# Laying the sums of expert weights over the steps: one split a step, half-size weight units, and a second output product that runs on through the set-up of the pairs

## The chip, the core and the metric

The kernel runs on one core of one Trainium2 chip. The core has TensorE (PE, matmuls, with a weight load in front of each), VectorE (DVE), ScalarE (ACT), GpSimd (POOL) and SyncE (SP), which here only issues DMAs. Tiles live in SBUF, matmul results in the eight banks of PSUM, tensors in DRAM. Each engine works through its own list in order and waits on semaphores for the others; SP's list is the DMA queue, so a DMA that must wait holds back all those behind it. The metric is the device time of one execution, as the median of several runs.

## The reference

Eight batches of attention with 12 heads, 448 positions and head size 64, where the heads are mixed before and after the softmax, and behind it a gated layer without nonlinearity over all 3584 rows:

```python
scores = scale * np.matmul(q, k.transpose(0, 1, 3, 2))
scores = np.einsum('bhij,hg->bgij', scores, w_pre)
attn = softmax(scores)                       # along the last axis
attn = np.einsum('bhij,hg->bgij', attn, w_post)
x = (attn @ v)  # to rows of 768
a = x @ w1; b = x @ w2                       # 768 x 1024 each
out = (a * b @ w3) @ w_out                   # 1024 x 1024, 1024 x 768
```

The weights of the layer arrive in double precision and are converted in the kernel.

## The kernel before, in words

**The steps.** `run` walks through 366 steps `n`. A step takes ten query rows of all twelve heads (120 partitions) through one stage each of a pipeline: `fetch` of the raw scores four steps ahead, `split_r` into a high and a low part two steps ahead (DVE L201, POOL L202), `mix` one ahead (PE L209 to L211), `softmax` (DVE L218, ACT L221), and behind it `scale` (DVE L230 to L233) and `post` (PE L241, with the copy L247 on ACT that empties the bank). One `mix` ends each step, so the 360 matmuls of L211 mark the steps in the trace; all stretches below are cut at their ends. Scores of later batches (L174, L175, store L183) and the product with `v` (L272) are spread over the steps by tables. A step with `av` work has 48 matmuls of L272 and no background work.

**The background.** Between these, `advance` issues matmuls of a background generator. `shares` gives each step its number, so that `count` matmuls lie evenly between two steps. First w3 and w_out are folded into one weight; then batches 0 and 1 go through the layer one by one (`expert_atoms`: hidden products L480 with w1 and w2, output product L507); then the other six batches go in three pairs with seven products in place of eight per block (`phases`, `layer`, L650), which need sums of blocks of the weights. Every value is split into two parts of lower precision, and a product takes three matmuls.

**The weights.** w1 and w2 are converted piece by piece in steps 52 to 102 (`converting`, DVE L104 to L108), put into tiles `wu` and stored to DRAM. Later units are loaded from there (`load_unit`, L351). `ask_units` appends a load to the list `later` as long as fewer than `w_ahead` units stand ready, and `do_later` issues that list on SP at the head of the next step, behind the row fetch.

**The sums.** While a weight passes for the last time unit by unit (the folded weight in batch 0's output product, w1 and w2 in batch 1's hidden product), `seen` adds the two parts of each unit into a tile `y` (L427), and when the two blocks are there, `sums` forms four sums with four operations (L441 to L446). `split` copies the high part on ACT (L453), forms the low part on POOL (L454) and appends the store `s_d`. Everything is dated: `at(delay, f)` puts `f` at a fixed number of steps after the unit passed, and `do_timed` runs all that is due in a step at once. The tiles `s` have three buffers, the tiles `y` four.

**The set-up of the pairs.** At `PAIR` (step 190) the background of the single batches must be done (`shares(LATE, PAIR - 1, ...)` ends at step 188). Pools are closed and opened again over the same memory, the x of two batches is loaded in four steps (`load`, L566), the first three splits follow, and the pairs' matmuls begin at `P_AT`, step 196.

Of the kernel before, what the change touches and what calls it, by code (L numbers as in the profile page):

```python
# [27 lines left out]
NS = 50  # L28
# [13 lines left out]
class Kernel:  # L42
# [297 lines left out]
    def units(self):  # L340
        return [u for b in range(ONE) for u in
                [(w, f, 0) for f in self.order(KF, b == 1) for w in range(2)] +
                [(3, d, q) for d in self.order(K1, b == 0) for q in range(2)]]

    def order(self, n, summed):

        return [i + j for i in range(n // 2) for j in (0, n // 2)] if summed else range(n)

    def load_unit(self):
        t, view, src = self.unit_from(f"wu{self.n_loaded}", *self.unit_list[self.n_loaded])  # L350
# [5 lines left out]
    def unit_of_one(self, name, w, f, q):  # L356
        t, h = self.wp.tile([128, K1, 2, 128], F32R, tag="w", name=name), KF // 2
        if w < 2:
            return t, t, self.w_d[w][f]
        return t[:, :h], t[:, :h], self.w34_d[f][:, q * h:(q + 1) * h]  # L360

    def unit_of_pair(self, name, w, f, m):
        h, c = (K1 // 2, KF // 2) if w < 2 else (KF // 2, K1 // 2)
        t = self.wp.tile([128, KF // 2 * 256], F32R, tag="w", name=name)[:, :h * 256]
        src = self.w_d[w] if w < 2 else self.w34_d
# [5 lines left out]
    def unit_jobs(self):  # L371

        h = K1 // 2
        for w, f, _ in self.unit_list[:2 * KF]:
            src = self.w_src[w].rearrange("(k p) f -> p k f", p=128)
            for q in range(2):
                yield src[:, q * h:(q + 1) * h, f * 256:(f + 1) * 256], lambda x, w=w, f=f, q=q: self.unit_part(x, w, f, q)

    def unit_part(self, x, w, f, q):
        h = K1 // 2  # L380
        if q == 0:
            self.unit = self.wp.tile([128, K1, 2, 128], F32R, tag="w", name=f"wu{self.n_loaded}")
            self.loaded.append(self.unit)
            self.n_loaded += 1
        t = self.unit
        self.two_parts(x, *(t[:, q * h:(q + 1) * h, i] for i in range(2)))
        if q:
            self.later.append(lambda: self.nc.sync.dma_start(self.w_d[w][f], t.bitcast(F32)))
# [577 lines left out]
```

## Time and profile before

| | us |
|---|---|
| median of 3 runs | 1701.85 (1700.35 to 1702.36) |
| the profiled execution, its own time | 1705.28 |
| its span | 1703.5 |
| PE busy | 1601.2 (94%) |
| DVE busy | 1122.4 (66%) |
| POOL busy | 1078.5 (63%) |
| ACT busy | 932.3 (55%) |
| DMA, mean rate | 262 GB/s |

How to read it: busy time of PE counts matmuls that run at the low clock with their longer time, so the granted clock stands beside it. The two levels are 2.4 GHz (1.00) and 1.2 GHz (0.50); a stretch between them has a mean. The `idle before` of a group names the engine or DMA whose event ended the wait.

### The profile page before, as it was taken

The numbers are of one execution on the slowest core, as the hardware profiler recorded it, in microseconds if no ns is written. First come the engines' busy times: TensorE is split into PE (matmuls) and PEld (weight loads), VectorE is DVE, ScalarE is ACT, GpSimd is POOL, SyncE is SP. The second block draws the span as 40 slices with busy tenths as digits, with TensorE's granted clock in tenths as the row PEclk, the third lists the DMA queues.
The fourth block names the chain that finished last, engine by engine and source line by source line (L and its number), as shares of the span: only waits on it lengthen the run. The fifth ranks groups of instructions, "written<-read, shape, count | busy, mean of one in ns | idle before, by whom it ended". The sixth has DMA issues, their size and how long they took to land. (4 is left out here: it accounts for less than half of the span.)

```text
span 1703.5 us, 31656 instructions
## 1 busy us (share of the span) xinstructions
PE 1601.2 (94%) x10548; PEld 1433.5 (84%) x10548; DVE 1122.4 (66%) x2586; ACT 932.3 (55%) x2160; POOL 1078.5 (63%) x922
## 2 busy tenths in 40 slices
PE   4899998999999989989889999999999999999999
PEld 1479997888899878878689899989999899899988
DVE  4867666788758778763456666866665677844673
ACT  2777665677755555545555565565665444433221
POOL 1566554676656676764466777876775665746674
PEclk6999999999999999999889999999999999999999
DMA  7888778998989998878788888788987866679875
GB/s 254 284 259 278 241 220 247 292 309 277 278 260 311 335 300 284 283 260 278 231 252 259 284 253 261 235 263 283 325 272 231 251 204 194 201 209 323 278 236 180
DMA packets 228736, 446.09 MB, mean 262 GB/s; under 512 B 21214, under 2 KB 157662, under 8 KB 228574
## 3 DMA queue, kind: packets, MB, share of 16 engines
q1 hardware_dynamic: 228574, 444.07, 82.7%
q8 instruction: 84, 1.38, 0.4%
q14 instruction: 78, 0.64, 0.1%
HBM read 309.90 MB, written 134.09 MB: 261 GB/s over the span
## 5 line engine op out<-in xcount | busy, mean ns | idle before, releaser
L202 POOL TENSOR_TENSOR rl<-r,rh 120x448 fp32r<-120x448 f32 x360 | 436.8, 1213 | 438.2 <-DVE rh L201 146.4
L221 ACT ACTIVATE e<-psm,mn 120x448 f32<-120x448 f32 x360 | 228.8, 636 | 446.7 <-DVE sa L230 350.3
L218 DVE TENSOR_REDUCE mn<-psm 120x1 f32<-120x448 f32 x360 | 223.7, 621 | 367.7 <-PE psm L211 366.7
L241 PEld LDWEIGHTS pso<-w,e 120*112 120x112 f32 (+1 forms) x2880 | 350.4, 179 | 80.4 <-ACT mt L247 66.5
L241 PE MATMUL pso<-w,e 120*112 120x120 f32 (+1 forms) x2880 | 366.4, 271 | 43.8 <-ACT mt L247 43.7
L650 PE MATMUL e<-eh,wu 128*128 128x448 f32 x1008 | 304.2, 371 | 0.5 <-DVE c L604 0.5
L247 ACT COPY mt<-pso 112x480 f32<-112x480 f32 x360 | 206.4, 573 | 38.5 <-PE pso L241 37.8
L650 PEld LDWEIGHTS e<-eh,wu 128*128 128x128 f32 x1008 | 187.6, 189 | 15.3 <-DVE c L604 1.5
L201 DVE CAST rh<-r 120x448 fp32r<-120x448 f32 x360 | 177.0, 492 | 21.1 <-DMA r<-raw_d 18.2
L179 ACT COPY st<-psq 112x448 f32<-112x448 f32 x336 | 174.0, 528 | 30.7 <-DMA raw_d<-st 24.2
L650 PE MATMUL e<-el,wu 128*128 128x448 f32 x504 | 187.2, 371 | 3.3 <-POOL el L589 3.2
L233 DVE TENSOR_SCALAR w<-wpo,ri 120x120 f32<-120x120 f32 x360 | 164.6, 457 | 12.6
L209 PE MATMUL psm<-rh,wph 120*120 120x448 f32 x360 | 141.3, 392 | 23.0 <-DVE rh L201 23.0
L272 PE MATMUL psa<-mt,v 112*64 112x150 f32 (+1 forms) x2304 | 159.1, 295 | 0.6 <-DMA v<-v 0.6
L272 PEld LDWEIGHTS psa<-mt,v 112*64 112x64 f32 x2304 | 145.6, 138 | 7.2 <-DMA v<-v 1.0
L211 PE MATMUL psm<-rl,wph 120*120 120x448 f32 x360 | 134.2, 373 | 1.4 <-POOL rl L202 1.3
L604 DVE TENSOR_TENSOR c<-c,e 128x448 f32<-128x448 f32 x168 | 101.1, 615 | 52.2 <-PE e L650 47.5
L480 PE MATMUL eg<-xh,wu 128*128 128x448 f32 x384 | 130.3, 389 | 4.7 <-ACT wu L113 4.0
L164 POOL TENSOR_TENSOR ql<-kq,qh 128x448 fp32r<-128x448 f32 x84 | 98.0, 1167 | 56.7 <-ACT qh L162 56.2
L210 PE MATMUL psm<-rh,wpl 120*120 120x448 f32 x360 | 133.5, 371 | 0.0
L174 PE MATMUL psq<-kk,qh 128*112 128x448 f32 x336 | 126.3, 376 | 6.5 <-ACT st L179 6.1
L175 PE MATMUL psq<-kk,ql 128*112 128x448 f32 x336 | 124.5, 371 | 0.0
(114 smaller groups left out, 2903.4 us busy)
## 6 DMA issues: line engine op xcount, KB each, us to landing
r<-raw_d SPq DMA_DIRECT2D x352, 210.0 KB, 4.0
raw_d<-st SPq DMA_DIRECT2D x168, 392.0 KB, 4.6
wu<-s_d SPq DMA_DIRECT2D x96, 384.0 KB, 4.4
v<-v SPq DMA_DIRECT2D x144, 224.0 KB, 4.6
kq<-kq SPq DMA_DIRECT2D x42, 672.0 KB, 7.1
wu<-w_d SPq DMA_DIRECT2D x72, 384.0 KB, 5.6
wu<-w_d SPq DMA_DIRECT2D x51, 512.0 KB, 5.5
wu<-s_d SPq DMA_DIRECT2D x36, 512.0 KB, 4.3
```

What stands on the lines that cost most here:

```text
L179: copy(st[:, c % 2], p)
L201: nc.vector.tensor_copy(rh[:K], r[:K])
L202: nc.gpsimd.tensor_tensor(rl[:K], r[:K], rh[:K].bitcast(F32), op=ALU.subtract)
L209: nc.tensor.matmul(p[:K, :S], self.wph[:K, :K], rh[:K], start=True, stop=False)
L211: nc.tensor.matmul(p[:K, :S], self.wph[:K, :K], rl[:K], start=False, stop=True)
L218: nc.vector.tensor_reduce(mn[:K], p[:K, :S], axis=AX.X, op=ALU.min)
L221: nc.scalar.activation(e[:K], p[:K, :S], AF.Exp, bias=mn[:K], scale=-1.0, accum_out=sm[:K])
L233: nc.vector.tensor_scalar_mul(w2[:K, :, :w], wv[:K, :, :w], ri[:K])
L241: nc.tensor.matmul(p[:, j, :, :w], e[:K, j * JT:(j + 1) * JT], w2[:K, :, :w], start=True, stop=True)
L247: self.ends.append((4, lambda: copy(dst, p[:, :, :, :w])))
L272: nc.tensor.matmul(self.psa[rows, g % 3, :W], v[:, j, rows], mt[:, j, 2 * g + s, :W], start=(j == 0), stop=(j == NJ - 1))
L650: nc.tensor.matmul(p, w[:, k, x], ops[m, k][y], start=(k == 0 and t == 0), stop=(k == nk - 1 and t == 2))
```

## The change: what it does

- **Three queues in place of dates.** `jobs` holds additions of units, sums, and splits. `do_sums` runs at most one job of each queue in a step, and only jobs that were queued in an earlier step.
- **Sums wider and one fewer.** The four blocks of a weight lie in one tile `y` of 4 x 512 columns (two buffers). Three operations do what four did: two on two blocks at once, one on one.
- **Half-size units.** w1 and w2 are made, stored and loaded in halves, as the folded weight was; `wp` has five buffers of half the size and `w_ahead` is 3. In batch 1 the two blocks of w1 follow each other, then those of w2 (`hidden`), so that a group of sums is complete after two products.
- **One pool of tiles.** The small tiles of `expert_atoms` come from the same numbered tiles as those of the pairs (`take`, `give`); 20 of them exist from `SWITCH` on, 30 more from `PAIR` on.
- **The output product runs on.** `PAIR` is step 187, `P_AT` 195, and the shares of the single batches reach to step 194. One unit list and one generator cover single batches and pairs. `pair_setup` does the loads and first splits in seven steps beside the second batch's output product.

```diff
+    def hidden(self, b):
+        if b == 1:
+            return [(w, f + i) for f in range(KF // 2) for w in range(2) for i in (0, KF // 2)]
+        return [(w, f) for f in range(KF) for w in range(2)]
...
-    def at(self, delay, f):
-        self.timed.append((self.step + delay, f))
-
-    def do_timed(self):
-        now = [f for n, f in self.timed if n <= self.step]
-        self.timed = [x for x in self.timed if x[0] > self.step]
-        for f in now:
-            f()
+    def do_sums(self):
+
+        for jobs in self.jobs:
+            if jobs and jobs[0][0] < self.step:
+                jobs.pop(0)[1]()
...
         def whole():
-            if halves[0] == 0:
-                self.ys[w, f] = self.cb.tile([128, 2, 512], F32, tag="y", name=f"y{w}_{f}")
...
+            if (w, f % c) not in self.ys:
+                self.ys[w, f % c] = self.cb.tile([128, 4, 512], F32, tag="y", name=f"y{w}_{f}")
+            u = t.bitcast(F32)
+            x = self.ys[w, f % c][:, 2 * (f // c) + q, :k * 128].rearrange("p (k c) -> p k c", k=k)
+            self.nc.vector.tensor_tensor(x, u[:, :, 0], u[:, :, 1], op=ALU.add)
+            if f >= c and q == 1:
+                self.sums(w, f - c, k)
+
+        self.jobs[0].append((self.step, whole))
...
-            nc.vector.tensor_tensor(x[11], x[11], x[21], op=ALU.subtract)
-            nc.vector.tensor_tensor(x[21], x[21], x[22], op=ALU.add)
-
-        def second():
-            nc.vector.tensor_tensor(x[22], x[22], x[11], op=ALU.subtract)
-            nc.vector.tensor_tensor(x[12], x[12], x[22], op=ALU.subtract)
...
-        self.at(2, first)
-        self.at(3, second)
-        for delay, m, q in ((4, 7, 11), (4, 5, 21), (5, 6, 22), (6, 3, 12)):
-            self.at(delay, lambda m=m, q=q: split(m, q))
...
+        def first():
+            sum(y[:, 0:2], y[:, 0:2], y[:, 2:4], ALU.subtract)
+
+        def second():
+            sum(y[:, 1:3], y[:, 1:3], y[:, 0::3], ALU.add)
+            for m, i in ((5, 2), (3, 1)):
+                self.jobs[2].append((self.step, lambda m=m, i=i: split(m, i)))
+
+        def third():
+            sum(y[:, 3], y[:, 3], y[:, 0], ALU.subtract)
+            for m, i in ((6, 3), (7, 0)):
+                self.jobs[2].append((self.step, lambda m=m, i=i: split(m, i)))
+
+        self.jobs[1] += [(self.step, f) for f in (first, second, third)]
...
+    def pair_setup(self, phases):
+
+        loads = phases[0][0] + phases[1][0]
+        for step in (loads[:1], (), loads[1:2], phases[0][1], loads[2:3], (), loads[3:]):
+            for f in step:
+                f()
             yield
...
-        PAIR, P_AT = 4 * NB + 10, 4 * NB + 16
+        PAIR, P_AT = 4 * NB + 7, 4 * NB + 15
...
-        share |= shares(LATE, PAIR - 1, (E_1 + E_2) * ONE - E_1)
+        share |= shares(LATE, P_AT, (E_1 + E_2) * ONE - E_1)
...
-                self.wp = self.pool("wp", 3, side="right")
+                self.wp = self.pool("wp", 5, side="right")
+                self.up = self.pool("up", 1, side="right")
...
-                self.xq, self.cb = self.pool("xq", 2), self.pool("cb", 4)
+                self.xq, self.cb = self.pool("xq", 2), self.pool("cb", 2)
...
-                ahead = 1 if n < SWITCH else 2 * (done // (3 * K1) + 2 + (done > 0))
+                ahead = 1 if n < SWITCH else 2 * done // (3 * K1) + 4 + (done > 0)
```

How the instructions move, at three places. Names: `s0_0_6` is the split for product 6 of the first block of w1 (`s1_` of w2, `s2_` of the folded weight), `st` and `psq` are scores, `e139` and `pso137` belong to a row step, numbers at the end of a name count tiles.

First ACT's list around the splits of the first blocks of w1 and w2, steps 139 and 140, before:

```order
L221 ACTIVATE e139_7963,sm139_7964<-psm139_7950,mn139_7961 120x448
L492 CAST eh1_4_7936<-em1_4_7935 128x448
L179 COPY st4_2_2_7926<-psq4_2_3_7978 112x448
L453 CAST s0_0_3_7982<-y0_0_7456 128x384
L453 CAST s1_0_7_7985<-y1_0_7551 128x384
L453 CAST s1_0_5_7988<-y1_4_7798 128x384
L247 COPY mt3_0_7863<-pso137_7998 112x48x10
L221 ACTIVATE e140_8020,sm140_8021<-psm140_8007,mn140_8018 120x448
L179 COPY st4_3_0_8036<-psq4_3_0_8033 112x448
L453 CAST s1_0_6_8038<-y1_4_7798 128x384
```

and the same list of the changed kernel:

```order
L221 ACTIVATE e139_7953,sm139_7954<-psm139_7939,mn139_7951 120x448
L495 CAST eh1_0_7966<-em1_0_7943 128x448
L179 COPY st4_2_2_7920<-psq4_2_3_7970 112x448
L441 CAST s0_0_6_7975<-y0_0_7547 128x384
L247 COPY mt3_0_7858<-pso137_7982 112x48x10
L221 ACTIVATE e140_8004,sm140_8005<-psm140_7991,mn140_8002 120x448
L179 COPY st4_3_0_8020<-psq4_3_0_8017 112x448
L441 CAST s0_0_7_8023<-y0_0_7547 128x384
L247 COPY mt3_0_7858<-pso138_8026 112x48x10
```

Three copies in one step became one, and the splits of w2's block now come after those of w1's.

Second, DVE's list at step 135, where the sums of w2 begin, with the semaphores each waits for (`DMAHW` are DMA landings); `y1_0` is w2's sum tile, `y2_2` that of the folded weight's last block. The changed kernel:

```order
L201 CAST rh137_7741<-r137_7618 120x448 [waits DMAHW5_49,Pool_49]
L421 TENSOR_TENSOR y1_0_7749<-wu48_7571 128x384 [waits DMAHW5_49,DMAHW4_49,DMAHW7_49,DMAHW0_49,Pool_49]
L434 TENSOR_TENSOR y0_0_7547<-y0_0_7547 128x2x384
L218 TENSOR_REDUCE mn136_7777<-psm136_7767 120x1 [waits PE_49]
L230 TENSOR_SCALAR sa135_7782<-sm135_7733 120x1 [waits Activation_49]
L231 RECIPROCAL ri135_7783<-sa135_7782 120x1 [waits DVE_49]
L233 TENSOR_SCALAR w2135_7784<-wpo_136,ri135_7783 120x120 [waits DVE_49]
```

and SP's list of the changed kernel at the heads of steps 135 to 137, each from its row fetch on:

```order
L194 DMA r139_7724<-raw3_d_65 120x448
L446 DMA s2_6_d_91<-s2_2_6_7700 128x512
L447 DMA s2_6_d_91<-y2_2_7072 128x512
L357 DMA wu51_7728<-w1_d_71 128x768
L194 DMA r140_7772<-raw3_d_65 120x448
L183 DMA raw4_d_66<-st4_1_2_7697 112x2x448
L446 DMA s2_7_d_92<-s2_2_7_7752 128x512
L447 DMA s2_7_d_92<-y2_2_7072 128x512
L194 DMA r141_7816<-raw3_d_65 120x448
```

The last part of `y2_2` is stored at the head of step 136 and its landing is one of the four that L421 of step 135 waits for. The nearest case before is L427 of step 134:

```order
L231 RECIPROCAL ri133_7690<-sa133_7689 120x1 [waits DVE_49]
L233 TENSOR_SCALAR w2133_7691<-wpo_136,ri133_7690 120x120 [waits DVE_49]
L201 CAST rh136_7695<-r136_7572 120x448 [waits DMAHW2_49,Pool_49]
L427 TENSOR_TENSOR y0_4_7706<-wu30_7418 128x384 [waits DMAHW3_49,DMAHW7_49,DMAHW2_49,Pool_49]
...
L218 TENSOR_REDUCE mn135_7729<-psm135_7722 120x1 [waits PE_49]
L230 TENSOR_SCALAR sa134_7734<-sm134_7687 96x1 [waits Activation_49]
```

There the stores were issued at the heads of steps 132 and 133, so the wait reaches back and not forward.

Third, PE's list in the set-up, the step that ends with `psm191`, before:

```order
L174 MATMUL psq5_4_2_10656<-kk5_4_10444,qh5_4_10442 112x448
L175 MATMUL psq5_4_2_10656<-kk5_4_10444,ql5_4_10443 112x448
L241 MATMUL pso188_10661<-w2188_10590,e188_10536 112x120 x4
L209 MATMUL psm191_10666<-rh191_10594,wph_144 120x448
L210 MATMUL psm191_10666<-rh191_10594,wpl_145 120x448
L211 MATMUL psm191_10666<-rl191_10595,wph_144 120x448
```

and of the changed kernel, where `eo1_4` is a block of batch 1's output:

```order
L174 MATMUL psq5_4_2_10667<-kk5_4_10432,qh5_4_10430 112x448
L175 MATMUL psq5_4_2_10667<-kk5_4_10432,ql5_4_10431 112x448
L510 MATMUL eo1_4_10565<-eh1_3_9739,wu84_10201 128x448
L510 MATMUL eo1_4_10565<-el1_3_9740,wu84_10201 128x448
...
L510 MATMUL eo1_4_10565<-eh1_4_8140,wu85_10361 128x448
L241 MATMUL pso188_10676<-w2188_10604,e188_10539 112x120 x4
L510 MATMUL eo1_4_10565<-el1_4_8141,wu85_10361 128x448
...
L510 MATMUL eo1_4_10565<-eh1_5_8646,wu85_10361 128x448
L510 MATMUL eo1_4_10565<-el1_5_8647,wu85_10361 128x448
L209 MATMUL psm191_10685<-rh191_10608,wph_144 120x448
```

Eight background matmuls stand in a step that had none.

## Rows read from the trace of the kernel before

**Rows 1.** The page, part 1: busy us, share of the span, instructions.

```profile
PE 1601.2 (94%) x10548; PEld 1433.5 (84%) x10548; DVE 1122.4 (66%) x2586; ACT 932.3 (55%) x2160; POOL 1078.5 (63%) x922
```

**Rows 2.** Windows: length, busy of PE, PEld, DVE, ACT, POOL, clock, DMA share, GB/s.

```profile
285.00:478.70 193.70, 182.70 (x1265) 160.85 (x1264) 151.23 (x395) 136.91 (x325) 130.57 (x118) 1.00 0.91 283
478.70:524.70 46.00, 46.00 (x338) 42.45 (x337) 30.56 (x74) 27.25 (x64) 26.05 (x21) 1.00 0.88 273
524.70:602.30 77.60, 74.11 (x527) 66.31 (x526) 60.63 (x122) 43.23 (x101) 54.29 (x42) 1.00 0.98 328
602.30:625.90 23.60, 17.81 (x127) 15.77 (x126) 14.48 (x29) 13.50 (x34) 16.41 (x14) 0.93 0.84 287
625.90:647.20 21.30, 21.30 (x130) 19.70 (x129) 19.74 (x41) 13.24 (x33) 14.03 (x13) 1.00 0.92 294
647.20:692.90 45.70, 41.10 (x295) 37.21 (x294) 36.62 (x69) 24.64 (x60) 31.08 (x26) 0.96 0.87 281
692.90:737.00 44.10, 40.34 (x255) 36.33 (x254) 37.02 (x71) 24.75 (x59) 32.10 (x27) 0.92 0.85 278
737.00:761.40 24.40, 18.60 (x127) 16.74 (x126) 12.17 (x24) 12.57 (x30) 15.99 (x15) 0.86 0.83 281
761.40:828.00 66.60, 64.22 (x445) 58.56 (x444) 28.22 (x88) 35.66 (x83) 30.73 (x28) 1.00 0.79 252
828.00:859.80 31.80, 19.21 (x95) 14.98 (x94) 13.16 (x35) 15.24 (x36) 14.58 (x13) 0.71 0.83 262
```

**Rows 3.** Waits from 602.3 to 625.9: total us, times, longest.

```profile
ACT s L453 <- DMA s_d<-s: 7.1, 2, 4.5
PE pso L241 <- ACT mt L247: 5.8, 2, 5.1
```

**Rows 4.** Timeline in the same stretch: start, length, instruction, idle before.

```profile
615.96 1.94 PE L241 MATMUL pso<-w,e 120*112 120x120 f32 x8 [5.11 <-ACT mt L247]
621.44 0.51 ACT L453 CAST s<-y 128x384 fp32r<-128x384 f32 x1 [4.49 <-DMA s_d<-s]
```

**Rows 5.** Timeline of DVE and POOL around 607.

```profile
606.79 0.55 DVE L445 TENSOR_TENSOR y<-y,y 128x384 f32<-128x384 f32 x1
607.00 1.35 POOL L202 TENSOR_TENSOR rl<-r,rh 120x448 fp32r<-120x448 f32 x1 [0.52 <-PE psm L211]
607.37 1.40 DVE L446 TENSOR_TENSOR y<-y,y 128x384 f32<-128x384 f32 x1
```

**Rows 6.** Groups by form, 478.7 to 828.0: busy us, mean ns, idle before.

```profile
L427 DVE TENSOR_TENSOR y<-wu 128x384 f32<-128x384 f32 x32 | 35.9, 1162 | 1.1 <-DMA s_d<-y 1.1
L446 DVE TENSOR_TENSOR y<-y,y 128x384 f32<-128x384 f32 x8 | 11.1, 1390 | 0.3
L445 DVE TENSOR_TENSOR y<-y,y 128x384 f32<-128x384 f32 x8 | 6.3, 786 | 0.0
L446 DVE TENSOR_TENSOR y<-y,y 128x512 f32<-128x512 f32 x3 | 4.6, 1521 | 0.1
...
L454 POOL TENSOR_TENSOR y<-y,s 128x512 fp32r<-128x512 f32 x12 | 15.6, 1313 | 1.9 <-ACT s L453 1.9
```

**Rows 7.** DMA, 478.7 to 859.8: packets, MB, share; issues, us to landing.

```profile
q1 hardware_dynamic: 52202, 107.70, 86.9%
s_d<-s SPq DMA_DIRECT2D x32, 384.0 KB, 4.6
s_d<-y SPq DMA_DIRECT2D x12, 256.0 KB, 5.4
```

**Rows 8.** Waits of SP and PE, 828.0 to 859.8.

```profile
SPq L566 <- DMA out<-eos: 6.3, 1, 6.3
PE pso L241 <- ACT mt L247: 6.4, 4, 4.5
PE psm L209 <- DVE rh L201: 5.7, 1, 5.7
```

**Rows 9.** Timeline of DVE in the set-up.

```profile
845.11 0.39 DVE L201 CAST rh<-r 120x448 fp32r<-120x448 f32 x1 [8.61 <-DMA r<-raw_d]
```

More of the change, by code (lines that the diff above doesn't have):

```diff
@@ L419, in whole @@
         def whole():
-            if halves[0] == 0:
-                self.ys[w, f] = self.cb.tile([128, 2, 512], F32, tag="y", name=f"y{w}_{f}")
-            y = self.ys[w, f]
-            for i in halves:
-                u = t[:, i * k:(i + 1) * k] if w < 2 else t
-                u = u.bitcast(F32)
-                x = y[:, i, :k * 128].rearrange("p (k c) -> p k c", k=k)
-                self.nc.vector.tensor_tensor(x, u[:, :, 0], u[:, :, 1], op=ALU.add)
-        self.at(1, whole)
-        if f >= c and halves[-1] == 1:
-            self.sums(w, f - c, k)
@@ L455, in split @@
+            hi, lo = s[:, :n], s[:, n:2 * n] if w < 2 else x
+            nc.scalar.copy(hi.bitcast(F32R), x)
+            nc.gpsimd.tensor_tensor(lo.bitcast(F32R), x, hi, op=ALU.subtract)
             if w < 2:
@@ L472, in expert_atoms @@
[L472 to L491 removed]
+        nc, xs, hs, a = self.nc, self.xs.pop(b), {}, {}
@@ new lines, in expert_atoms, with first, second, parts @@
+        for n, (w, f) in enumerate(self.hidden(b)):
+            p = self.bank(6 + n % 2, f"eg{b}_{f}_{w}")[:, :S]
+            for k in range(K1):
+                if k % (K1 // 2) == 0:
+                    u = self.next_unit()
+                    if b == 1:
+                        self.seen(w, f, k // (K1 // 2), u)
+                for t, (x, y) in enumerate(PAIRS):
+                    nc.tensor.matmul(p, u[:, k % (K1 // 2), x], xs[y][:, k],
+                                     start=(k == 0 and t == 0), stop=(k == K1 - 1 and t == 2))
+                    yield
+            def first(f=f, p=p):
+                a[f] = self.take(f"ea{b}_{f}")
+                nc.scalar.copy(a[f], p)
+            def second(f=f, p=p):
+                m = self.take(f"em{b}_{f}")
+                nc.vector.tensor_tensor(m, a[f], p, op=ALU.mult)
+                self.give(a[f])
+                self.soon.append((None, lambda: parts(f, m)))
+            def parts(f, m):
+                h, l = hs[f] = [self.take(f"e{x}{b}_{f}", F32R) for x in "hl"]
@@ L492, in parts @@
                 nc.scalar.copy(h, m)
                 nc.gpsimd.tensor_tensor(l, m, h.bitcast(F32), op=ALU.subtract)
-            self.soon.append((None, parts))
-            hs[f] = h, l
+                self.give(m)
+            self.ends.append((6 + n % 2, second if w else first))
         self.do_ends()
@@ L693, in run @@
         self.later, self.ends, self.soon = [], [], []
-        self.slot, self.free, self.keep, self.x_made, self.n_groups = {}, list(range(NS)), [], [0] * B, 0
-        self.timed, self.ys, self.pairs = [], {}, False
+        self.slot, self.free, self.keep, self.x_made, self.n_groups = {}, list(range(N_UP)), [], [0] * B, 0
+        self.jobs, self.ys, self.pairs = [[], [], []], {}, False
         dp = self.pool("dram", 1, space=DRAM)
@@ L833, in run @@
                 self.close("xp0")
[L834 removed]
+                self.xq, self.cb = self.pool("xq", 2), self.pool("cb", 2)
             if n == PAIR:
[L836 to L837 removed]
+                assert done >= 2 * E_1 + E_2 and unit_pieces is None and not any(self.jobs) and not self.ys
                 self.do_ends()
```

149 lines of the change are left out of this document (57 added, 92 removed).

## The prediction

> **What bounds the kernel now.** I read the page's busy line first: TensorE (PE) works 1601 of 1703.5 us [rows 1], so a change of order can only win what PE idles or runs at the lower clock. Then I cut the trace into stretches at the ends of the L211 matmuls, one per step, and read each row of the windows as "length less busy time times granted clock": that is what the stretch lost against PE at full clock. From 478.7 to 859.8 us (steps 107 to 195) the rows give 0.0, 3.5, 7.0, 0.0, 6.2, 7.0, 8.4, 2.4 and 18.2 [rows 2]. The reader is to see four short stretches that lose 28.6 us together (602.3, 647.2, 692.9 and 737.0), one that loses 18.2 (828.0 to 859.8), and between them stretches with none. The sum is 52.7 us. The stretch before, 285.0 to 478.7, loses 11.0, but the change hardly touches it.
>
> Next come the waits of one of the four [rows 3] and its timeline [rows 4]. ScalarE (ACT) waits 7.1 us for stores `s_d<-s`. Its copies at L453 take three buffers in turn, and in steps 139 to 141 six of them follow closely (the first of the order pieces): the fourth wants a buffer whose store has only just been issued. Behind L453 on ACT stands L247, which empties the bank that PE's L241 wants, so PE idles 5.1 us, and the stretch's mean clock falls to 0.93, between the full 2.4 GHz and the level of 1.2. The other three stretches have the same L453 pile in the program, in steps 149 to 152, 159 to 162 and 169 to 171.
>
> The set-up of the pairs has another cause. In steps 189 to 195 PE has no background matmuls, and SyncE (SP), whose queue is in order, stands 6.3 us at the first L566 load: its tile lies where the output tile `eos` lay, whose store has not landed [rows 8]. The row fetches queue behind it, VectorE's (DVE) L201 waits 8.6 us for one [rows 9], and PE waits 5.7 for L201 and 6.4 for L247 [rows 8]. The clock falls to a mean of 0.71 [rows 2].
>
> **The change, part by part.**
>
> 1. *Splits one per step.* Queue 3 gives one L441 copy, one GpSimd (POOL) subtraction and one store per step. A buffer comes back after three steps, some 10 us, against a landing of 4.6 us [rows 7]. So the four piles go: 28.6 us is the most that this can win. I also count the 5.9 us of the stretches at 524.7 and 761.4 as removable, since the doubled additions and the late output units stand there.
>
> 2. *Sums wider and one fewer.* For each of the 11 groups four operations become three, two of them twice as wide. A narrow one takes 0.79 us or, behind POOL, 1.39 [rows 6]; the form of 512 columns takes 1.52, so 384 more columns cost about (1.52 - 1.39) x 3 = 0.4 us, an estimate. Old group: 2 x 0.79 + 2 x 1.39 = 4.4. New group: between 3 x 0.79 + 0.8 = 3.2 and 3 x 1.39 + 0.8 = 5.0. Over 11 groups that is -13 to +7 us of DVE time, which matters only where DVE is late. With 28.6 us of waiting gone the same work must fit a shorter time: DVE was busy 180.7 of the 236.7 us from 524.7 to 761.4 (six rows), and 32.1 us of that were lost, so it would fill 180.7 of 204.6, 88%. The stretch at 625.9 had DVE at 93% and lost nothing; the one at 285.0 had it at 78%, in runs of conversions, and lost 5.7%, which here would be 12 us. I take 7, with 0 and 12 as ends: the work is laid evenly now, but one step with a whole addition and a wide sum still asks more of DVE than PE needs.
>
> The rows show DVE and POOL excluding each other: L446 ends 1.40 us after it started, just behind POOL's L202, though L445, the same size, took 0.55 [rows 5]. The Trainium skill ("SBUF — State Buffer", "SBUF: two separate sides") says that a DVE operation with two SBUF inputs and a GpSimd operation take one port pair in turn, each for its whole length, and this trace agrees. By that rule POOL's 163.9 us from 524.7 to 761.4 and 88 such operations at 0.55 add to 212 us, and the wider sums (0.95 each) make it 215, against 204.6 of PE: this term would be 10 and the time 1671.
>
> 3. *A new wait.* Sums now live in two buffers of 4 x 512 where four of 2 x 512 stood. For the output weights the low part is stored from the sum's own tile. In the second of the order pieces DVE's L421 of step 135 writes `y1_0` over `y2_2`, whose last part ACT and POOL split in the same step and SP stores at the head of step 136. DVE must then wait for POOL (1.31 us [rows 6]) and the landing (5.4 us [rows 7]), 6.7 us; behind it on DVE stand the reduction, the row scale and the cast of step 136, which ACT, POOL and PE need one step later. Before had a milder wait of this kind, 1.1 us at L427 [rows 6]. PE has some two steps in hand, but DVE also has a wide sum queued there and the clock falls after an idle. ACT's waits of 7.1 us cost their stretch 7.0 [rows 2, 3]. I take 8; ends 1 and 12.
>
> 4. *Set-up under the output product.* Steps 187 to 194 now carry 6 to 8 matmuls each of the second batch's output, so the work PE lacked is there, and the first loads go to free tiles and not over `eos`. The removable loss is 18.2. The loads and splits are as many as before, spread over seven steps instead of five, but from 478.7 to 859.8 the queues move 107.70 MB [rows 7], and in 381.1 - 52.7 = 328.4 us that is 328 GB/s. The best rows are 328 at a DMA share of 0.98, which lost 3.5, and 312 GB/s would be 345 us, 17 late. I take 3, ends 0 and 17.
>
> 5. *Half-size units, three ahead.* The same bytes in 32 more transfers; the conversions of w1 and w2 keep their steps but for a few pieces that move one to three steps in the stretch at 285.0. PE covers an issue, and each load still stands two to six steps ahead of its use: 0, between a gain of 2 and a loss of 2.
>
> 6. *Shares.* The 576 background matmuls of the first two batches now lie over 88 steps, not 82; PE's total is unchanged. Nothing.
>
> **Sum.** Removable 52.7; new 7 + 8 + 3 = 18; net 34.7. The profiled execution took 1705.28 us, 3.4 over the median of 1701.85. 1705.3 - 34.7 = 1670.6, less 3.4: 1667, and I say **1668**.
>
> **Rivals.**
>
> *All of it goes.* DVE's wait at step 135 is hidden by the two steps in hand, and the even laying keeps DVE and the queues ahead: for it speaks the stretch at 625.9, against it that 328 GB/s must hold throughout. Then 52.7 less 2: 1651.
>
> *The queues set the pace.* Once ACT no longer waits, transfers are late instead: row fetches land after their step and DVE waits at L201, as in [rows 9], but often. For it: DMA shares of 0.92 to 0.98 where nothing stalled. Against: half-size units need no more bytes. At 295 GB/s the stretch takes 107.70 / 0.295 = 365 us, 16 less than 381: 1686.
>
> *Slower.* The same mechanism with no gain left: the bursts at 602.3 to 761.4 had 278 to 287 GB/s, and if the queues give 278 whatever ACT does, the stretch takes 387 us and the kernel 1708. It decides from 107.70 / 381.1 = 283 GB/s downward. Against it stands 524.7 to 602.3, where 328 were moved.
>
> *The change does not do what it says:* the first x loads or the fetches behind them wait for something else at the set-up, so its 18.2 stay while the piles go. Then the net is 16 and the time 1685; the order shows no such wait, and I count it with the second rival.
>
> **How the numbers follow.** The forecast (1655 to 1682) has 0.62, all of it goes 0.13, the queues or an unhidden set-up 0.19, slower 0.06. The range 1649 to 1688 takes the forecast, most of the first rival and most of the second. Within 0.2% (3.4 us), about what a measurement of this kernel can tell from no change, lies the thin edge between the second and third: 0.02. So faster 0.92, same 0.02, slower 0.06.
>
> **What would show it.** Right: no ACT wait at the split copies for `s_d`; PE busy through the set-up at full clock; one DVE wait for `s_d` near step 135 with PE idle some 5 to 8 us after it. Wrong: DVE waiting at L201 for `r` over many steps (the queues), PE waiting for `wu` loads (units too late), POOL waits for DVE across the sums stage costing over 12 us, or the set-up still showing a clock near 0.7.

## The result, and the profile after

The changed kernel takes **1677.02 us** (median of four runs, 1672.98 to 1678.15) against 1701.74 for the kernel before beside it: a ratio of 0.9845, 95% interval 0.983 to 0.986. The forecast was 1668, inside a range of 1649 to 1688. The profiled execution of the changed kernel took 1676.97 us, with a span of 1675.2.

The page's busy line answers to [rows 1]: PE has 10.6 us less of busy time, since fewer of its matmuls ran at the lower clock, in a span that is 28.3 us shorter. The other engines do nearly the same work.

```profile
PE 1590.6 (95%) x10548; PEld 1425.6 (85%) x10548; DVE 1112.0 (66%) x2575; ACT 931.3 (56%) x2160; POOL 1081.9 (65%) x922
```

The windows answer to [rows 2], cut at the ends of the same L211 matmuls (those of 647.2 and 692.9 begin at 646.0 and 687.6 here). Columns as there: length, busy time of PE, PEld, DVE, ACT, POOL, clock, DMA share, GB/s. The last row is one step, number 137, out of the third.

```profile
283.60:478.90 195.30, 185.16 (x1269) 162.82 (x1268) 151.81 (x398) 135.95 (x325) 132.15 (x119) 0.99 0.89 282
478.90:523.70 44.80, 44.80 (x331) 41.08 (x330) 28.51 (x71) 27.83 (x65) 26.32 (x21) 1.00 0.93 284
523.70:609.80 86.10, 73.74 (x517) 66.58 (x516) 59.43 (x119) 45.36 (x105) 57.00 (x43) 0.94 0.88 289
609.80:625.20 15.40, 15.40 (x125) 14.21 (x124) 9.16 (x24) 9.72 (x24) 10.41 (x10) 1.00 0.97 324
625.20:646.00 20.80, 20.80 (x127) 19.04 (x126) 20.04 (x40) 14.89 (x36) 17.75 (x14) 1.00 0.95 313
646.00:687.60 41.60, 38.34 (x290) 34.72 (x289) 30.38 (x65) 24.59 (x59) 31.65 (x27) 1.00 0.94 306
687.60:728.70 41.10, 37.83 (x249) 34.42 (x248) 32.79 (x66) 24.41 (x58) 29.65 (x26) 0.96 0.88 280
728.70:744.20 15.50, 15.50 (x125) 14.26 (x124) 11.62 (x26) 9.74 (x24) 10.14 (x9) 1.00 1.00 342
744.20:806.60 62.40, 61.98 (x435) 56.84 (x434) 35.54 (x93) 38.11 (x90) 41.27 (x35) 1.00 1.00 331
806.60:832.00 25.40, 24.81 (x150) 22.63 (x149) 13.57 (x36) 16.41 (x39) 15.29 (x14) 1.00 1.02 341
591.70:609.80 18.10, 7.68 (x63) 6.69 (x62) 8.73 (x15) 5.09 (x12) 6.62 (x5) 0.72 0.60 203
```

Read as in the prediction (length less busy time times clock), steps 107 to 195 lose 0.0, 16.8, 0.0, 0.0, 3.3, 4.8, 0.0, 0.4 and 0.6: 25.9 us where 52.7 were lost. Those 26.8 us are nearly all of the 28.3 between the two profiled executions. The pile stretches of [rows 2] lose nothing in two places (609.8 and 728.7) and 8.1 us in the other two, and the set-up runs at full clock. But the third row, which lost 3.5 us before, now loses 16.8, of which 12.6 in one step.

Below, the loss of a single step is its length less what its matmuls take where nothing waits: 0.207 us for a background matmul, and 1.84 for the step's own 13 (5.24 in the steps that also run L272). By this finer measure steps 107 to 195 lost 55.7 us before and 24.7 after: 12.9 in step 137, 5.1 in 165, 2.2 in 154, 2.5 in 124 and 125, 1.5 in 150, and 0.7 in the set-up (24.9 in all; other steps come out a few tenths under the measure). The step that ends with `psm138` is step 137.

The waits of step 137, from 591.7 to 609.8 (total us, times, longest):

```profile
ACT e L221 <- DVE sa L230: 12.3, 1, 12.3
DVE y L421 <- DMA s_d<-y: 11.6, 1, 11.6
POOL rl L202 <- issue: 11.1, 1, 11.1
PE pso L241 <- ACT mt L247: 10.4, 1, 10.4
```

And the timeline around it, DVE, POOL, SP's queue and PE, a few rows of each (start, length, instruction, idle before and its releaser):

```profile
587.12 0.38 DVE L201 CAST rh<-r 120x448 fp32r<-120x448 f32 x1
599.10 0.56 DVE L421 TENSOR_TENSOR y<-wu 128x384 f32<-128x384 f32 x1 [11.60 <-DMA s_d<-y]
599.58 0.95 DVE L434 TENSOR_TENSOR y<-y 128x768 f32<-128x768 f32 x1
...
605.08 1.49 DVE L421 TENSOR_TENSOR y<-wu 128x384 f32<-128x384 f32 x1
...
588.62 1.15 POOL L202 TENSOR_TENSOR rl<-r,rh 120x448 fp32r<-120x448 f32 x1
589.73 1.28 POOL L442 TENSOR_TENSOR y<-y,s 128x512 fp32r<-128x512 f32 x1
...
604.98 1.17 POOL L165 TENSOR_TENSOR kk<-kq,kk 64x448 fp32r<-64x448 f32 x1
...
593.26 0.34 SPq L447 DMA_DIRECT2D s_d<-y  x1
...
602.74 1.94 PE L241 MATMUL pso<-w,e 120*112 120x120 f32 x8 [10.42 <-ACT mt L247]
```

This is the wait of the prediction's third step: L421 of `y1_0` writes over `y2_2`, whose low part is split by POOL's L442 and stored by L447. DVE is ready at 587.50. POOL ends the split at 591.01 (3.5 us), SP has issued the store at 593.60 (2.6), and DVE goes on at 599.10 (5.5). Behind L421 stand the wide sum and the reduction that ACT, and through L247 PE, wait for.

Waits from 478.9 to 806.6, those on the sums' buffers alone; no wait of ACT's split copies (L441) for `s_d` is left, where [rows 3] had 7.1 us in one stretch:

```profile
DVE y L421 <- DMA s_d<-y: 14.5, 2, 11.6
DVE y L421 <- POOL s L442: 8.7, 2, 4.3
```

DVE's additions and sums by form, 478.9 to 806.6, answer to [rows 6] (busy us, mean ns, idle before):

```profile
L434 DVE TENSOR_TENSOR y<-y 128x768 f32<-128x768 f32 x16 | 24.8, 1548 | 0.0
L421 DVE TENSOR_TENSOR y<-wu 128x384 f32<-128x384 f32 x32 | 23.3, 729 | 20.3 <-DMA s_d<-y 11.6 <-POOL s L442 8.7
L434 DVE TENSOR_TENSOR y<-y 128x1024 f32<-128x1024 f32 x6 | 9.2, 1540 | 0.0
L434 DVE TENSOR_TENSOR y<-y 128x384 f32<-128x384 f32 x8 | 9.1, 1144 | 0.0
L434 DVE TENSOR_TENSOR y<-y 128x512 f32<-128x512 f32 x3 | 2.0, 683 | 0.0
```

The sums take 45.1 us, 4.1 for a group. The additions take 0.73 us each where L427 took 1.16 [rows 6]: 6 of the 32 last over 1 us, where 21 did, as with one addition a step they stand less often beside a POOL operation (0.56 us at 599.10 with POOL idle, 1.49 at 605.08 beside L165). Half of what they win goes again on the same engine: the 80 casts L201 take 45.5 us where they took 39.3.

The queues, 478.9 to 832.0, answer to [rows 7]:

```profile
q1 hardware_dynamic: 54413, 107.57, 93.1%
s_d<-s SPq DMA_DIRECT2D x32, 384.0 KB, 5.1
s_d<-y SPq DMA_DIRECT2D x12, 256.0 KB, 4.9
```

The same bytes as before in 353.1 us and not 381.1. The landings of the splits are within half a microsecond of the old ones; the loads of v take 5.7 us where they took 4.6.

### The profile page after: what moved, and what is told of

Read it like the earlier page. It is cut to its first block, busy times and chain, and to the rows that moved or that the text cites. A ratio compares the mean times of both kernels' runs of the same rounds, so it can differ in the third digit from the quotient of the medians.

```text
span 1675.2 us, 31720 instructions
## 1 busy us (share of the span) xinstructions
PE 1590.6 (95%) x10548; PEld 1425.6 (85%) x10548; DVE 1112.0 (66%) x2575; ACT 931.3 (56%) x2160; POOL 1081.9 (65%) x922
## 5 line engine op out<-in xcount | busy, mean ns | idle before, releaser
L202 POOL TENSOR_TENSOR rl<-r,rh 120x448 fp32r<-120x448 f32 x360 | 444.2, 1234 | 416.3 <-issue 130.5
L221 ACT ACTIVATE e<-psm,mn 120x448 f32<-120x448 f32 x360 | 228.8, 635 | 438.9 <-DVE sa L230 359.8
L218 DVE TENSOR_REDUCE mn<-psm 120x1 f32<-120x448 f32 x360 | 223.8, 622 | 337.0 <-PE psm L211 336.2
L241 PEld LDWEIGHTS pso<-w,e 120*112 120x112 f32 (+1 forms) x2880 | 346.5, 178 | 68.1 <-ACT mt L247 54.8
L241 PE MATMUL pso<-w,e 120*112 120x120 f32 (+1 forms) x2880 | 362.0, 269 | 33.3 <-ACT mt L247 31.1
L247 ACT COPY mt<-pso 112x480 f32<-112x480 f32 x360 | 206.7, 574 | 34.4 <-PE pso L241 33.7
L179 ACT COPY st<-psq 112x448 f32<-112x448 f32 x336 | 174.0, 528 | 25.4 <-DMA raw_d<-st 22.7
L201 DVE CAST rh<-r 120x448 fp32r<-120x448 f32 x360 | 182.5, 507 | 2.9 <-DMA r<-raw_d 2.7
L233 DVE TENSOR_SCALAR w<-wpo,ri 120x120 f32<-120x120 f32 x360 | 165.0, 458 | 12.6
L272 PE MATMUL psa<-mt,v 112*64 112x150 f32 (+1 forms) x2304 | 158.2, 294 | 1.2 <-DMA v<-v 1.2
L272 PEld LDWEIGHTS psa<-mt,v 112*64 112x64 f32 x2304 | 144.8, 138 | 7.5 <-DMA v<-v 1.4
L211 PE MATMUL psm<-rl,wph 120*120 120x448 f32 x360 | 133.2, 370 | 1.7 <-POOL rl L202 1.6
```

Of the source, the lines that this page charges most:

```text
L179: copy(st[:, c % 2], p)
L201: nc.vector.tensor_copy(rh[:K], r[:K])
L202: nc.gpsimd.tensor_tensor(rl[:K], r[:K], rh[:K].bitcast(F32), op=ALU.subtract)
L211: nc.tensor.matmul(p[:K, :S], self.wph[:K, :K], rl[:K], start=False, stop=True)
L218: nc.vector.tensor_reduce(mn[:K], p[:K, :S], axis=AX.X, op=ALU.min)
L221: nc.scalar.activation(e[:K], p[:K, :S], AF.Exp, bias=mn[:K], scale=-1.0, accum_out=sm[:K])
```

## The experiments

Each kernel was timed beside the kernel before on its own chip; the ratios are to that kernel. The changed kernel once more, without an edit (`again`), says how far such ratios carry:

> The changed kernel once more, unaltered, beside the runs of this call: it says how far its time of 1677 carries from one chip and hour to the next, since the narrow sums came out 7 us above it. If that was the sums, this run is at 1677 within 3 us; if it was the chip, at 1681 or more.

Measured: 1677.46 us (1675.3 to 1679.84), ratio 0.9846 (0.9833 to 0.9859). The change's gain is the same from chip to chip.

The losses in the table are those of the one profiled execution, by steps, in the finer measure. That execution can be one of the faster of its kernel: in pile_s7 it took 1662.7 us against a median of 1669.2, in gap 1678.6 against 1683.8, in pile 1685.3 against 1688.9; the others lie within about 3 us of their medians. `again`, profiled too, lost 13.7 us in step 137, 4.8 in 165 and 2.2 in 154.

| kernel | us, median | ratio (95%) | lost in steps 107 to 188 | in 189 to 195 |
|---|---|---|---|---|
| third_y | 1663.7 | 0.9773 (0.9755 to 0.9791) | 11.4 | 0.9 |
| v_first | 1662.1 | 0.9756 (0.9741 to 0.9771) | 9.9 | 3.6 |
| v_first2 | 1664.7 | 0.9789 (0.9765 to 0.9813) | 13.8 | 0.1 |
| pile_s7 | 1669.2 | 0.9793 (0.9772 to 0.9815) | 14.2 | 1.0 |
| changed | 1677.0 | 0.9845 (0.983 to 0.986) | 24.0 | 0.7 |
| burst | 1679.5 | 0.9863 (0.9842 to 0.9885) | 26.3 | 3.8 |
| gap | 1683.8 | 0.9902 (0.9887 to 0.9918) | 25.4 | 6.9 |
| gap_burst | 1684.1 | 0.9893 (0.9873 to 0.9913) | 26.0 | 9.4 |
| narrow | 1684.4 | 0.9888 (0.9872 to 0.9904) | 31.9 | 0.0 |
| pile | 1688.9 | 0.9921 (0.9904 to 0.9939) | 33.7 | 1.8 |
| early2 | 1700.4 | 0.9993 (0.9983 to 1.0003) | 36.1 | 16.1 |
| early | 1702.5 | 1.0001 (0.9986 to 1.0016) | 37.9 | 20.2 |
| before | | 1 | 37.2 | 18.5 |

### third_y: another buffer for the sums

```
-        self.ys[w, f % c] = self.cb.tile([128, 4, 512], F32, tag="y", name=...)
+        third = w < 2 and (2 * f + w) % 3 == 0
+        self.ys[w, f % c] = self.cb.tile([128, 4, 384 if third else 512], F32,
+                tag="y1" if third else "y", name=..., bufs=1 if third else 2)
```

To make room, the two tiles of the conversions (`m` and `x` in `to_f32`) moved to a pool of their own, which is closed at LATE.

> The changed kernel with a third buffer for the sums of the hidden weights (every third group of them has a buffer of its own), so that a group's first addition no longer writes over the group whose last split has only just run. Theory (what is left to lose in the sums stage is reuse of the two y buffers): the DVE waits at the first addition of y1_0, y0_2 and y0_3 go, with the 12.9, 2.2 and 5.1 us that steps 137, 154 and 165 lose now; the wait for y2_0's store at steps 124 and 125 (2.5 us) stays, since the output weights' sums keep two buffers. 1677 - 20 = 1657 us (1653 to 1662). Rival (the queues or DVE are saturated there, and the wait only shows where the lateness collects): the waits move to the row fetches (DVE waiting for r) or to other DVE work, and at most half is won: 1667 or more.

Measured: 1663.7 us, a ratio of 0.9773, 0.7% under that of the changed kernel with intervals apart. The losses of steps 137 and 154 went, step 165 fell from 5.1 to 0.5. Of the 20 us expected 13 came, so the time is just above the theory's range. The rest shows in the windows of the stretch that was 523.7 to 609.8, of step 137, and of step 140:

```profile
522.70:595.50 72.80, 71.18 (x517) 64.53 (x516) 59.49 (x118) 45.18 (x105) 55.99 (x42) 1.00 0.96 320
590.30:595.50 5.20, 5.20 (x63) 4.75 (x62) 5.13 (x7) 2.93 (x7) 5.04 (x5) 1.00 1.03 367
602.50:611.90 9.40, 6.96 (x63) 6.42 (x62) 2.48 (x6) 2.79 (x8) 4.63 (x5) 0.82 1.04 348
```

The stretch is 13.3 us shorter and step 137 takes 5.20 us where it took 18.1. Step 140 now loses 4.1, and steps 166 and 167 another 2.3. In step 140 PE waits for a load of v, which is on PE's timeline there:

```profile
606.38 4.91 PE L272 MATMUL psa<-mt,v 112*64 112x148 f32 x48 [2.44 <-DMA v<-v]
```

So the buffers were the cause of these three losses. That the stall had been giving the queues time, which they now lack in step 140, is a reading of mine that no run shows by itself. The rival, that no more than half would be won, is out: 13 of 20.

### v_first and v_first2: the loads of v ahead of the stores

```
-        self.later.append(self.load_v)
+        self.later.insert(0, self.load_v)                                          # v_first
+        self.later.insert(len(self.later) if self.pairs else 0, self.load_v)       # v_first2
```

Both are third_y with this one line changed.

> The kernel with the third y buffer, and the loads of v issued ahead of the split's store at the head of a step. Theory (of the 20 us that third_y should have won, 4.1 came back at step 140, where PE waits 2.4 us for v: SP issues in order, and the v loads stand behind a store that waits for POOL's split): the store of 0.85 us and its wait are out of their way, the v loads start 1 to 1.5 us sooner, and step 140 loses 1.5 or less: 1661 us (1657 to 1665). Rival (the loads land late because the queues are full, not for their place): PE's wait for v stays over 2 us, 1664.

Measured: 1662.1 us. Step 140 lost 0.9, so its place in SP's queue was what made v late:

```profile
601.66 3.24 PE L272 MATMUL psa<-mt,v 112*64 112x148 f32 x48 [0.88 <-DMA v<-v]
```

But step 191 lost 3.7 where third_y had lost 1.1, and steps 144 to 146 lost 2.0.

> The kernel 'v_first' with the loads of v ahead of the stores only up to the set-up of the pairs, since step 191, where third_y lost 1.1 us, lost 3.7 with them ahead. Theory (their place in SP's queue): step 140 still loses 1 or less and step 191 is back at 1: 1660 us (1656 to 1664). Rival (such losses of a few us move about with the load on the queues, whatever stands first): as much is lost in another step and the time is that of third_y, 1662 to 1665.

Measured: 1664.7 us. Step 191 lost next to nothing, as expected; step 140 lost 1.4, over the 1 expected, and 131 and 176 now lose 1.5 and 1.9. The rival holds: the intervals of third_y and of these two all overlap, so the order of SP's queue gave nothing that can be measured. Losses of one or two microseconds move about.

### pile and pile_s7: the splits not spread

```
-        for jobs in self.jobs:
-            if jobs and jobs[0][0] < self.step:
+        for i, jobs in enumerate(self.jobs):
+            while jobs and jobs[0][0] < self.step:
                 jobs.pop(0)[1]()
+                if i < 2:
+                    break
```

> The changed kernel with the splits of queue 3 run two at a time (all that are due in a step) and not one per step; sums, units and set-up as in the changed kernel. Theory: two things pull apart. The last split of a group runs two steps sooner, so the waits of DVE on y buffers shrink (step 137 from 12.9 us lost to some 2, steps 154 and 165 to about none), -15 to -18. ACT's wait for s_d stores comes back, since the fourth split of a group wants the buffer of the first, whose store was issued about one step before: 1 to 4 us at each of 11 groups, of which PE feels about half, +6 to +20. Net 1665 (1658 to 1680). Rival (spreading the splits was itself the gain, as my first step says, at the full 28.6 us): ACT waits at four piles come back at their old 7 us each and the time is 1690 or more.

Measured: 1688.9 us, 0.8% above the changed kernel, so half of the change's gain is gone; the expectation of 1665 was wrong. As expected, step 137 fell to 4.1 and steps 154 and 165 lost almost nothing. But ACT's waits came back and cost more than that won. ACT's groups by form, 476.9 to 814.3:

```profile
L443 ACT CAST s<-y 128x384 fp32r<-128x384 f32 x32 | 15.8, 521 | 17.1 <-DMA s_d<-s 12.7 <-POOL s L444 2.3 <-POOL rl L202 1.6
L443 ACT CAST s<-y 128x512 fp32r<-128x512 f32 x12 | 7.2, 626 | 6.3 <-DMA s_d<-s 6.3
```

They wait 23.4 us in all, 19.0 of it in eight waits for `s_d`. The longest, 4.72 us, is in step 126, which loses 1.2; the dearest is in step 155 (ACT's timeline):

```profile
672.80 0.51 ACT L443 CAST s<-y 128x384 fp32r<-128x384 f32 x1 [3.55 <-DMA s_d<-s]
```

Steps 126, 134, 145, 151, 155, 162, 167, 176 and 178 together lose 23, and in all of them but 176 one of ACT's split copies waits, most often for `s_d`: ACT's wait holds L247, and PE with it, and the clock falls on top (a mean of 0.84 in step 155).

> The splits two at a time as in the kernel 'pile', and the fourth split of a group (m = 7) with a buffer of its own, so that it no longer wants the buffer of the group's first split. Theory (pile lost 12 us because ACT's fourth copy waited some 3.5 us for a store issued a step before, while the last split, two steps earlier, won back most of the waits on the y buffers): ACT's wait for s_d goes, the losses of steps 126, 134, 145, 151, 155, 162, 167, 176 and 178 (23 us together in pile) go with it, and the loss at step 137 stays near 4: 1689 - 23 = 1666 us (1660 to 1673), faster than the changed kernel though nothing is spread over steps. Rival (two splits in a step are themselves too much for ACT or POOL): 1680 or more with no s_d wait on ACT.

The edit, on top of pile and with the tiles of the conversions moved as in third_y:

```
+            pool, tag, bufs = (self.cb, "s7", 1) if m == 7 else (self.cs, "s", 3)
-            s = self.cs.tile([128, CW, 2], I32, tag="s", name=..., bufs=3)
+            s = pool.tile([128, CW, 2], I32, tag=tag, name=..., bufs=bufs)
```

Measured: 1669.2 us, ratio 0.9793 (0.9772 to 0.9815). ACT's split copies wait for nothing, 474.2 to 792:

```profile
L444 ACT CAST s<-y 128x384 fp32r<-128x384 f32 x32 | 15.0, 526 | 0.0
L444 ACT CAST s<-y 128x512 fp32r<-128x512 f32 x12 | 6.9, 629 | 0.0
```

So what cost in `pile` was the fourth copy's wait for a store of the first, and one more buffer cures it as well as spreading does. With that buffer the unspread kernel is faster than the changed one, since its last split comes two steps earlier and the sums' buffers are free in time (step 137 loses 2.6). This settles the mechanism that the first step of the prediction names, and that spreading has a price: it holds the sums' buffers longer. Whether the kernel before lost its time by that mechanism is another question (see below).

### narrow: the wide sums as narrow ones

```
-            sum(y[:, 0:2], y[:, 0:2], y[:, 2:4], ALU.subtract)
+            sum(y[:, 0], y[:, 0], y[:, 2], ALU.subtract)
+            sum(y[:, 1], y[:, 1], y[:, 3], ALU.subtract)
```

and the addition of `second` in the same way.

> The changed kernel with the two wide sums written as four narrow ones (five operations for a group, in the same steps). Theory (DVE's time for the sums is off the path but for the stall at step 137): no difference, 1677 within 3 us, DVE busy up by at most some 10 us in all. Rival (wide operations hold the memory side shared with POOL longer, or short ones cost DVE time that the path feels): a change of over 4 us either way.

Measured: 1684.4 us, a ratio of 0.9888, 0.4% above the changed kernel with intervals apart: the rival's result. DVE's sums, 478.3 to 813.5:

```profile
L434 DVE TENSOR_TENSOR y<-y 128x384 f32<-128x384 f32 x40 | 42.6, 1098 | 0.0
L434 DVE TENSOR_TENSOR y<-y 128x512 f32<-128x512 f32 x15 | 14.5, 1002 | 0.0
```

57.1 us against 45.1, and steps 107 to 188 lose 8 us more, most in steps 125, 144, 145 and 176. DVE's sums are on the path after all: 12 us of them cost some 7.

### gap, burst and gap_burst: the set-up of the pairs

```
-        share |= shares(LATE, P_AT, (E_1 + E_2) * ONE - E_1)
+        share |= shares(LATE, PAIR + 2, (E_1 + E_2) * ONE - E_1)                   # gap, gap_burst
-        for step in (loads[:1], (), loads[1:2], phases[0][1], loads[2:3], (), loads[3:]):
+        for step in (loads[:1], loads[1:2], loads[2:3], loads[3:], phases[0][1]):  # burst, gap_burst
```

> The changed kernel with the second batch's output product ended two steps after the set-up begins and not eight, so that steps 189 to 194 have no background matmuls; the same matmuls stand closer in the steps before. Theory (PE needs work there, since the first operands' loads and the row fetches share the queues and come late): row fetches late, DVE waiting for r, PE idle and its clock at the lower level in steps 192 to 195; 7 to 16 us lost, 1688 us (1683 to 1694). Rival (the loss of before was SP's wait for the eos store alone, which does not come back): those steps take some 2.3 us each with PE busy, as steps 189 to 192 of before did, and the time is 1680 or less.

Measured: 1683.8 us, in the theory's range, but 6.9 us lost in steps 189 to 195 is just under its 7 and far under the 18.5 of before. By itself, with the loads spread, missing work makes about a third of that loss (6.9 less 0.7). And the wait that the theory names is not there: DVE waits for no row fetch in these steps, where L201 waited 16.5 us for them in the kernel before. Of the 6.9 us, 4.5 are lost in step 191, behind a copy of scores on ACT that waits for an earlier store of scores, with L247 and PE behind it (first line; the second is that of gap_burst, in the same steps):

```profile
ACT st L179 <- DMA raw_d<-st: 2.0, 1, 2.0
ACT st L179 <- DMA raw_d<-st: 5.5, 1, 5.5
```

> The changed kernel with the first operands' loads of the pairs in the first four steps of the set-up and their splits in the fifth, as the kernel before had them, with the output product running on beside them. In early2 the set-up still lost 16.1 us without any wait for the eos store, in gap 6.9 with the loads spread over seven steps. Theory (the loads crowded into few steps push the row fetches back, but steps of 3.5 us that have background matmuls hide most of it): steps 187 to 195 lose 2 to 6 us where they lost 1 in the changed kernel: 1680 us (1677 to 1684). Rival (the crowding alone makes the loss of before): 10 us or more lost there, 1687 or more.

Measured: 1679.5 us and 3.8 us lost, 3.1 more than in the changed kernel, as much as the theory said; the time alone can't be told from the changed kernel's, as the intervals overlap. Here too L201 waits for no row fetch; nearly all of the loss is in step 191, where L179 waits 4.3 us.

> The kernel 'gap' (no background matmuls in steps 189 to 194) with the loads in the first four steps, as in 'burst'. Theory (crowded loads and missing work make the loss together; the four loads of units that before had to begin anew at this place add the rest): 9 to 14 us lost in steps 187 to 195, against 6.9 in gap and 16.1 in early2: 1687 us (1683 to 1693). Rival (where the loads stand does not matter, before lost the rest by the units beginning anew): 6 to 8 us lost, the time of gap, 1684.

Measured: 1684.1 us, 9.4 us lost in the set-up: at the theory's lower end there, 7.0 of it in step 191. DVE waits for one row fetch, 2.6 us. In the time it can't be told from gap.

### early and early2: the wait for the last output tile

Both are the kernel before, with one line changed; early2 adds two more in `advance`. They leave steps 185 to 188 without background matmuls as well:

```
-        share |= shares(LATE, PAIR - 1, (E_1 + E_2) * ONE - E_1)
+        share |= shares(LATE, PAIR - 5, (E_1 + E_2) * ONE - E_1)                   # early, early2
+            if done == total and n > LATE:                                         # early2
+                next(background, None)
```

> The kernel before the change, with the second batch's output product ended four steps sooner (its matmuls stand closer in the steps ahead), so that the last output tile is stored before the first loads of the set-up. Theory (of the 18.5 us that the set-up lost in before, the wait of SP at its first load for the eos store made some 12, and missing work for PE some 6, as steps 189 to 195 of the kernel 'gap' show with 6.9): no SP wait for out<-eos, 6 to 8 us lost in steps 189 to 195, 1702 - 11 = 1691 us (1686 to 1696). Rival (PE without work and the burst of loads are what cost, the eos wait is hidden beside them): 14 us or more still lost there, 1698 or more.

Measured: 1702.5 us, no difference. This told nothing on the wait, because it stayed:

```profile
SPq L566 <- DMA out<-eos: 6.6, 1, 6.6
```

The last output tile's copy and store are queued only when the background is resumed at PAIR, however early its matmuls end.

> The kernel 'early' once more, with what was missing in it: the last output tile of the second batch is now copied out and stored as soon as its matmuls are through, four steps before the set-up, and not when the set-up begins (in 'early' the store still went out at 831 us, and SP waited 6.6 us for it as in before). Theory (the eos wait is some 12 of the 18.5 to 20 us lost in steps 189 to 195): no SP wait for out<-eos, those steps lose 6 to 9, 1691 us (1687 to 1696). Rival (no work for PE and the burst of loads are what cost): 14 us or more still lost there, 1698 or more.

Measured: 1700.4 us, ratio 0.9993. SP no longer waits for `eos`; its longest waits in 824.3 to 853.3 are others:

```profile
SPq L194 <- POOL rl L202: 3.2, 2, 1.7
SPq L194 <- DMA r<-raw_d: 2.7, 3, 1.9
```

Yet DVE's L201 still waits 11.9 us for row fetches, and 16.1 us are lost in the set-up (the clock is at 0.79):

```profile
824.30:853.30 29.00, 18.81 (x95) 14.21 (x94) 13.02 (x35) 16.17 (x38) 15.98 (x14) 0.79 0.97 300
```

The theory that the wait made 12 us falls: it made 2 to 4 (18.5 in before and 20.2 in early, against 16.1; early is the closer comparison, as it lacks the same background work). Once it is gone, the row fetches are late all the same, among the same loads, at a DMA share of 0.97.

## Why the prediction was right, and where it was not

**What bounds it, and the first step (the splits): the amount right, the cause right for two of the four stretches.** The waits of ACT's copies for `s_d` are gone, and pile and pile_s7 show both sides: three buffers and unspread splits bring them back, a fourth removes them. But I had read the waits of one stretch and taken the other three to be like it. In the kernel before, ACT's split copies wait for `s_d` 7.1 us in the stretch at 602.3 and 6.5 in the one at 737.0, but only 1.4 at 692.9 and not at all at 647.2. There, ACT's L221 waits for DVE's reduction L218 (before, 647.2 to 676.4 and 692.9 to 717.7):

```profile
ACT e L221 <- DVE mn L218: 5.7, 3, 3.4
ACT e L221 <- DVE mn L218: 6.2, 2, 4.4
```

The reduction starts late because DVE has first to end two sums and two additions of the same step, one right behind the other from 655.43 to 660.00, and again from 700.38 to 705.93. The end of the first pile (DVE's and ACT's timelines):

```profile
657.31 2.77 DVE L427 TENSOR_TENSOR y<-wu 128x384 f32<-128x384 f32 x2
660.00 0.61 DVE L218 TENSOR_REDUCE mn<-psm 120x1 f32<-120x448 f32 x1
660.64 0.63 ACT L221 ACTIVATE e<-psm,mn 120x448 f32<-120x448 f32 x1 [3.42 <-DVE mn L218]
```

Behind L221 stand L247 and PE, which idles 2.6 and 3.1 us. So of the 28.6 us only some 15.4 (7.0 and 8.4) stood behind the splits, and the other 13.2 behind DVE's own pile, which the queues of additions and sums take apart, not that of the splits. From 478.7 to 828.0 ACT waited 19.7 us for `s_d` and as much for L218; after, none and 2.3. No run spreads DVE's work alone, so how the gain divides between the queues is not shown.

**The second step (wide sums, one fewer): its price of 7 was too high.** DVE's sums came to 4.1 us for a group, between the 3.2 and 5.0 given. Apart from the waits on buffers, DVE's lateness shows in step 150 (1.5 us, and 1.7 before) and little else. Its reasoning was half right: narrow shows that DVE time does count here, 7 us for 12, and the two piles above show the same of the kernel before. But the additions, alone in their steps, became shorter by 12.6 us in all, which I had not seen, and the casts L201 longer by 6.2. The result of 1671 by the Trainium skill's rule ("SBUF — State Buffer", "SBUF: two separate sides") rested on a term of 10 where some 1.5 were lost, so it is nearer to the measured time by chance. What the Trainium skill states there, that such operations of DVE and GpSimd take one port pair in turn, each for its whole length, this trace agrees with in the lengths: L434 over 768 columns takes 0.95 us with POOL idle (599.58), and 1.55 in the mean.

**The third step (the new wait): this is where it went wrong, in size.** "DVE must then wait for POOL (1.31 us [rows 6]) and the landing (5.4 us [rows 7]), 6.7 us; ... I take 8; ends 1 and 12." The wait is at that place and of that kind, and the landing was 5.5. But POOL was 3.5 us behind DVE, not one split, and SP issued the store 2.6 us after it: 11.6 us in all, and step 137 loses 12.9. The same pair of buffers also makes DVE wait 4.3 us twice for POOL's last split (steps 154 and 165, 7.3 us lost) and 2.9 us for a store (124 and 125, 2.5 lost). I had priced one wait of three kinds. Together the reuse costs 22.7 us where 8 stood. third_y took all but 0.5 of the 20.2 in steps 137, 154 and 165 away and won 13.

**The fourth step (the set-up): the sum right, the cause wrong.** 18.2 us went, and 0.7 are lost where I took 3. But I put the loss to "its tile lies where the output tile `eos` lay, whose store has not landed". early2 shows 2 to 4 us for that. Missing work for PE is worth 6.2 (gap against the changed kernel) and the crowding of the loads 2.5 to 3.1 (gap_burst against gap, burst against the changed kernel), both for the most part behind L179's wait for a store, which the kernel before has too (5.3 us). The late row fetches of before (L201 waits 16.5 us for them there, 11.9 in early2) did not come back in these three, but for one wait of 2.6 us in gap_burst. What makes them late stays open, and with it some 7 us between gap_burst (9.4) and early2 (16.1). Two things differ that no run tried by itself: the kernel before begins four unit loads anew at this place, and all its loads of x stand in steps without background work, where gap_burst has two of the four beside it.

**The fifth step and the rivals.** PE waited for no unit after step 107. The queues didn't set the pace: they moved 107.57 MB at a share of 93.1%, with up to 342 GB/s where nothing was lost. "All of it goes" (1651) needed the third step to be hidden, and it was not.

**The numbers.** The new costs were 18 and came to 24.9 by the steps named: 14.7 more in the third, 5.5 less in the second, 2.3 less in the fourth. So the profiled execution took 1676.97 where the sum said 1670.6. That it came so near is in part luck: the second and fourth were priced 7.8 too high, which hides half of what the third lacked, and the 28.6 of the first went although half of it had another cause. And I took 3.4 off, as the profiled execution of before lay that much over its median; the one of after lies on its median.

## What to carry to other kernels

Read the waits of every stretch that is counted as gain, not of one for all: two of four piles that look alike in the program had another wait behind them. When a pile is spread over steps, each piece holds its input buffers longer: list every tile that the last piece still reads or is stored from, and ask who writes it next. Price such a wait from where the engines really stand (POOL was 3.5 us behind DVE) and with the in-order issue of the store, not from the durations alone. And a wait that a queue shows at the head of a stall is not its size: removing it (early2) gave 2 to 4 of 18 us, because what stood behind it was late for other reasons too.

## What the runs showed of the hardware that was not expected

The 16 DMA engines moved 331 to 342 GB/s from 728.7 to 832.0 with PE at full clock and at most 0.6 us lost in a window; I had taken 328, the best row of mine, for about the limit, though the kernel before had moved 338 from 550 to 600. And the length of a DVE addition of 384 columns depends more on where it stands than on its work: 0.56 us alone and 1.49 beside a POOL operation, so that laying the 32 of them one to a step took their mean from 1.16 to 0.73 us (and half of that went to the casts L201, 0.49 to 0.57 us in the mean).
